# Attention values beside ones columns, grouped scores, and another order of the expert matmuls, in a fused attention and MoE kernel

## The chip, the cores and the metric

The kernel runs on one core of a Trainium2 chip. The metric is device time in microseconds of one execution, as the median of several runs. A profiled execution gives the trace; its span runs from the first to the last instruction, and its own time is the span with what lies around it.

## What is computed

Inputs are q, k, v of shape (4 batches, 8 heads, 768 positions, 64), two expert weights and two scalars. Attention is banded: each query sees the first 8 keys and the last 96 positions, with a distance bias per head. Its output, 3072 rows of 512, goes through one expert.

```python
scores = scale * q @ k.T                        # per batch and head
keep = (pos_k < 8) | ((rel >= 0) & (rel < 96))
scores = where(keep, scores - slope[h] * dist, -1e9)
a = exp(scores - max); a = a / (sum(a) + 1e-9)
x = (a @ v) as (3072, 512)
h = x @ w_in                                    # 512 x 2048
g = s * relu(h)**2 + b
out = g @ w_out                                 # 2048 x 512
```

## The kernel before, in words

The work is cut into 12 granules j of 256 rows (three per batch), and each granule into 4 head pairs: 48 units u. Only one core works; the order on each engine comes from the order of the program text, rearranged by a scheduler that lets ready work pass work that waits, mostly at the start.

A unit passes through three stages. `stage_T` (lines 204 and 212) transposes two 128-row blocks of k and of q on TensorE into one PSUM bank, and VectorE copies them to SBUF (line 222); lines 226 to 229 put together the key block that reaches back (`koff`). `stage_S` (line 268) computes scores with the 64-row half of each head, so that the two heads of the pair run side by side in the two halves of the array's rows; ScalarE takes the exponential (line 278) and VectorE multiplies by a template that holds bias and mask (line 282). The eight templates are made once by ScalarE (line 163) from `base` (lines 153 to 157). `stage_A` computes values (line 316) with 64 weight columns per head, the two heads side by side in the two halves of the array's columns, and then the row sums in the same way with a block of ones as the weights (line 329). ScalarE takes the logarithm of the sums and the exponential of its negative (lines 339, 341), and VectorE multiplies (line 342) into `xT`.

The expert runs in chunks on finished granules. `moe_p1` (line 355) makes 256 of the 2048 hidden columns with 8 matmuls of 256 columns; ScalarE applies relu (line 363), VectorE squares (line 364) into `gT`. `moe_p2` (line 389) is half of a 128-row output block, 8 matmuls of 512 columns; after the second half VectorE applies s and the bias vector (line 398) and SP stores. The bias vector is b times the column sums of w_out: `emit_bvec` (line 371) sums them with 16 matmuls by ones.

The main loop has one step for each unit: scores of the next unit, a first-layer chunk, values of this unit, another chunk, transposes of the unit after next, half an output block. The first layer lags one granule, the second two. PSUM has 3 banks for scores, 2 for values, 3 shared by transposes, both expert layers and the bias vector.

All loads are on the POOL queue and cast f32 to bf16. Their order is: q, k, v of granule 0 (line 80), w_in in four parts (line 92), granule 1, w_out in four parts (line 98), granule 2, and one later granule per four steps. Eight transfers of this queue may be under way; the ninth waits for the first. VectorE makes `voff` (lines 192, 194) once per granule, the V block that reaches back.

Of the kernel before, what the change touches and what calls it, by code (L numbers as in the profile page):

```python
# [8 lines left out]
F32 = mybir.dt.float32  # L9
BF16 = mybir.dt.bfloat16  # L10
ACT = mybir.ActivationFunctionType
ALU = mybir.AluOpType
# [5 lines left out]
def kernel(  # L18
# [13 lines left out]
    nc = tc.nc  # L32
    P = nc.NUM_PARTITIONS

    B, H, S, D = q.shape
    NG = int(n_global)
    NL = int(n_local)
    DM = H * D
    DF = moe_w_in.shape[1]
    GB = 2  # L40
    GT = GB * P
    NGR = S // GT
    HP = H // 2
    KC = DM // P
    FC = DF // P
    NJ = B * NGR
    NU = NJ * HP
# [7 lines left out]
    const = ctx.enter_context(tc.tile_pool(name="const", bufs=1))  # L55
    ldp = ctx.enter_context(tc.tile_pool(name="ldp", bufs=2))
    qkp = ctx.enter_context(tc.tile_pool(name="qkp", bufs=2))
    work = ctx.enter_context(tc.tile_pool(name="work", bufs=3))
    ppool = ctx.enter_context(tc.tile_pool(name="ppool", bufs=8))
    gpool = ctx.enter_context(tc.tile_pool(name="gpool", bufs=2))  # L60
    xpool = ctx.enter_context(tc.tile_pool(name="xpool", bufs=3))
    ps_sc = ctx.enter_context(tc.tile_pool(name="ps_sc", bufs=3, space=bass.MemoryType.PSUM))
    ps_av = ctx.enter_context(tc.tile_pool(name="ps_av", bufs=2, space=bass.MemoryType.PSUM))
    ps_h = ctx.enter_context(tc.tile_pool(name="ps_h", bufs=3, space=bass.MemoryType.PSUM))

    nc.scalar.preload_act_table_set("natural_log_exp_and_others")


    nat = {}
    for b in range(B):  # L70
        for nm in ("q", "k", "v"):
            nat[nm, b] = None

    def load(nm, src, b, g, h0, nh):
        key = (nm, b)
        if nat[key] is None:
            nat[key] = ldp.tile([P, S // P, H, D], BF16, name=f"{nm}nat", tag=f"{nm}nat")
        t = nat[key]
        for sb in range(g * GB, (g + 1) * GB):
            nc.gpsimd.dma_start(  # L80
                t[:, sb, h0 : h0 + nh, :],
                src[b, h0 : h0 + nh, sb * P : (sb + 1) * P, :].rearrange("h p d -> p h d"),
            )

    w_in_bf = const.tile([P, KC, DF], BF16, name="w_in_bf")
# [13 lines left out]
            w_out_bf[:, i * w : (i + 1) * w, :], w_out_view[:, i * w : (i + 1) * w, :]  # L99
        )  # L100

    def load_granule(b, g, parts=1):
        n = H // parts
        for h0 in range(0, H, n):
            load("k", k, b, g, h0, n)
            load("q", q, b, g, h0, n)
            load("v", v, b, g, h0, n)

    s_bc = const.tile([P, 1], F32, name="s_bc")
    nc.sync.dma_start(s_bc[:], moe_s.to_broadcast((P, 1)))  # L110
# [2 lines left out]

    ident_bf = const.tile([P, P], BF16, name="ident_bf")
    make_identity(nc, ident_bf[:])
    ones_bf = const.tile([P, P], BF16, name="ones_bf")
    nc.vector.memset(ones_bf[:], 1.0)


    base = const.tile([P, 5, P], F32, name="base")  # L120
# [14 lines left out]
        fill=NEG_BIG,  # L135
# [9 lines left out]
        base=NL - 1,  # L145
        channel_multiplier=1,
    )
    load_granule(0, 0)
    for i in range(4):
        load_w_in(i, 4)  # L150

# [14 lines left out]
        tmpl.append(t)  # L166

    load_granule(0, 1)
    for i in range(4):
        load_w_out(i, 4)  # L170
    load_granule(0, 2)


    st = {}
    qk = {}
    xT = {}
# [8 lines left out]

    def make_voff(j):
        b, g = divmod(j, NGR)
        vn = nat["v", b]
        if g == 0:
            return  # L190
        vo = work.tile([P, GB, H, D], BF16, name="voff", tag="voff", bufs=2)
        nc.vector.tensor_copy(vo[:], vn[:, g * GB - 1 : (g + 1) * GB - 1, :, :])
        for i in range(GB):
            nc.vector.tensor_copy(vo[0:NG, i, :, :], vn[0:NG, 0, :, :])
        voff_tiles[j] = vo
# [45 lines left out]
    def stage_S(u):  # L241
# [43 lines left out]

        return mms, [lambda: post(0), lambda: post(1)]

    def stage_A(u):
        j, hp, b, g = unit(u)
        first = g == 0  # L290
        pts = st[u]["pt"]
        vn = nat["v", b]
        vo = None if first else voff_tiles[j]
        av = ps_av.tile([P, 4 * P], F32, name="ps_av", tag="av")
        if j not in xT:
            xT[j] = xpool.tile([P, KC, GT], BF16, name="xT", tag="xT")
        if first:
            dcol, ocol = (0, 1), (None, 2)
        else:
            dcol, ocol = (0, 3), (1, 2)  # L300

        def mms():
            for i in range(GB):
                for off in range(2):
                    c = (ocol if off else dcol)[i]
                    if c is None:
                        continue
                    for hi in range(2):
                        h = 2 * hp + hi
                        if not off:  # L310
                            vv = vn[:, g * GB + i, h, :]
                        elif first:
                            vv = vn[:, 0, h, :]
                        else:
                            vv = vo[:, i, h, :]
                        nc.tensor.matmul(  # L316
                            av[hi * D : (hi + 1) * D, i * P : (i + 1) * P],
                            lhsT=vv,
                            rhs=pts[hi][:, c * P : (c + 1) * P],
                            start=not off,  # L320
                            stop=bool(off) or ocol[i] is None,
                        )
            for i in range(GB):
                for off in range(2):
                    c = (ocol if off else dcol)[i]
                    if c is None:
                        continue
                    for hi in range(2):
                        nc.tensor.matmul(  # L329
                            av[hi * D : (hi + 1) * D, GT + i * P : GT + (i + 1) * P],  # L330
                            lhsT=ones_bf[:, 0:D],
                            rhs=pts[hi][:, c * P : (c + 1) * P],
                            start=not off,
                            stop=bool(off) or ocol[i] is None,
                        )

        def norm():
            lg = work.tile([P, GT], F32, name="lg", tag="lg")
            nc.scalar.activation(lg[:], av[:, GT : 2 * GT], ACT.Ln)  # L339
            rc = work.tile([P, GT], F32, name="rc", tag="rc")  # L340
            nc.scalar.activation(rc[:], lg[:], ACT.Exp, scale=-1.0)  # L341
            nc.vector.tensor_tensor(xT[j][:, hp, :], av[:, 0:GT], rc[:], ALU.mult)  # L342

        return mms, norm

    def moe_p1(j, fp):

        if j not in gT:
            gT[j] = gpool.tile([P, FC, GT], BF16, name="gT", tag="gT")
        g = gT[j]  # L350
        ps = ps_h.tile([P, 2, GT], F32, name="ps_1", tag="psh")
        for i in range(2):
            fc = 2 * fp + i
            for kc in range(KC):
                nc.tensor.matmul(  # L355
                    ps[:, i, :],
                    lhsT=w_in_bf[:, kc, fc * P : (fc + 1) * P],
                    rhs=xT[j][:, kc, :],
                    start=(kc == 0),
                    stop=(kc == KC - 1),  # L360
                )
        gs = g[:, 2 * fp : 2 * fp + 2, :]
        nc.scalar.activation(gs, ps[:], ACT.Relu)  # L363
        nc.vector.tensor_tensor(gs, gs, gs, ALU.mult)  # L364

    bvec = const.tile([P, DM], F32, name="bvec")

    def emit_bvec():
        ps = ps_h.tile([P, DM], F32, name="ps_b", tag="psh")
        for fc in range(FC):  # L370
            nc.tensor.matmul(  # L371
                ps[:],
                lhsT=ones_bf[:],
                rhs=w_out_bf[:, fc, :],
                start=(fc == 0),
                stop=(fc == FC - 1),
            )
        nc.vector.tensor_scalar_mul(bvec[:], ps[:], b_bc[:])

    po_cur = {}  # L380
# [26 lines left out]
            nc.sync.dma_start(out[t0 : t0 + P, :], o_sb[:])  # L407


    pend_loads = []  # L410
    for b in range(1, B):
        for g in range(NGR):
            pend_loads.append((b, g))

    def run_T(u):
        ops, evac = stage_T(u)
        for op in ops:
            op()
        evac()

    def run_S(u):
        mms, posts = stage_S(u)
        mms()
        for p_ in posts:
            p_()

    NSTEP = NU + 2 * HP
    run_T(0)
    run_T(1)
    run_S(0)  # L430
    for s in range(NSTEP):
        jm = s // HP
        qd = s % HP
        if qd == 0:
            if jm >= 0 and pend_loads:
                load_granule(*pend_loads.pop(0))
            if jm + 1 < NJ:
                make_voff(jm + 1)
        if s + 1 < NU:
            run_S(s + 1)  # L440
        if 1 <= jm <= NJ:
            moe_p1(jm - 1, 2 * qd)
        if s < NU:
            mms, norm = stage_A(s)
            mms()
            norm()
        if 1 <= jm <= NJ:
            moe_p1(jm - 1, 2 * qd + 1)
        if s + 2 < NU:
            run_T(s + 2)  # L450
        if s == HP + 2:
            emit_bvec()
        if 2 <= jm:
            moe_p2(jm - 2, qd // 2, qd % 2)


# [33 lines left out]
```

The softmax here doesn't subtract the row's maximum and nothing guards it: scores larger than these inputs give would overflow.

## Time and profile before

| what | us |
|---|---|
| median of 3 runs | 264.14 (263.92 to 265.49) |
| profiled execution, own time | 265.33 |
| its span | 263.5 |
| TensorE busy | 242.9 |
| VectorE busy | 152.7 |
| ScalarE busy | 144.7 |
| GpSimd busy | 71.1 |
| mean granted TensorE clock | 0.996 |

How to read it: PE is TensorE, PEld its weight loads, DVE VectorE, ACT ScalarE, POOL GpSimd, SP the store queue. A timeline line gives the start, the time that the merged instructions took, the engine, the line of the kernel, output and inputs with shapes, and a count; in brackets stands the idle time ahead and what ended it. The chain of waits follows the last instruction back, at each step to what released it. Matmuls overlap, so that their cost is read from the distance between starts and not from the duration of one.

### The profile page before, as it was taken

Reading aid. Unit: us, or ns where it says so; the run is one execution under the profiler, and the core shown is the slowest. Engines: PE = TensorE matmul, PEld = TensorE weight load, DVE = VectorE, ACT = ScalarE, POOL = GpSimd, SP = SyncE. Lnnn points to the kernel's source line nnn. Section 1 sums busy time; section 2 is a strip of 40 time slices with the busy share of each in tenths; the row PEclk is TensorE's granted clock in tenths of the full one; section 3 lists DMA queues with packets and bytes.
Section 4 is the critical chain, followed back from the end, with each engine's and each line's share of the span. In section 5 each row is a group of like instructions: output and inputs, shape, how many; then the busy total and the mean of one; then the engine's idle time right before and its main releaser. Section 6 shows DMA issues by size and latency. Waiting matters only on the chain.

```text
span 263.5 us, 5861 instructions
## 1 busy us (share of the span) xinstructions
PE 242.9 (92%) x2376; PEld 155.4 (59%) x2416; DVE 152.7 (58%) x441; ACT 144.7 (55%) x297; POOL 71.1 (27%) x89
## 2 busy tenths in 40 slices
PE   0573999999999999999999999999999999999993
PEld 0352565756666566666666666656666566666641
DVE  2440746777856676577575676567657567543331
ACT  4770454857557476575665756646556466463310
POOL 9945649859910000069700000000000000000000
PEclk9999999999999999999999999999999999999998
DMA  6999999999991100159990110110011011011112
GB/s 43 145 206 167 206 182 155 151 110 141 160 141 40 44 29 14 40 36 164 179 106 0 44 40 2 40 42 21 21 40 44 0 42 44 0 42 40 40 42 80
DMA packets 82875, 20.31 MB, mean 77 GB/s; under 512 B 75680, under 2 KB 79776, under 8 KB 82848
## 3 DMA queue, kind: packets, MB, share of 16 engines
q0 software_dynamic: 79104, 13.64, 69.3%
q1 hardware_dynamic: 3744, 6.29, 6.5%
q8 instruction: 19, 0.31, 0.5%
q14 instruction: 8, 0.07, 0.1%
HBM read 27.26 MB, written 6.29 MB: 127 GB/s over the span
## 4 chain that ended last, share of the span: by engine, by line
PE 89%; DMA 5%; POOL 3%; issue 1%; DVE 0%; ACT 0%; POOLq 0%
PE ps_s L268 6%; PE ps_av L316 6%; DMA knat<-in_k_dram 5%; PE ps_av L329 4%; PE ps_t L204 2%; PE ps_t L212 2%; PE ps_3986 L389 1%; PE ps_4006 L389 1%; PE ps_3944 L389 1%; PE ps_3006 L389 1%; PE ps_1081 L389 1%; PE ps_b L371 1%; PE ps_2048 L389 1%; PE ps_3880 L389 1%; PE ps_3793 L389 1%; PE ps_3642 L389 1%
## 5 line engine op out<-in xcount | busy, mean ns | idle before, releaser
L278 ACT ACTIVATE pt<-ps_s 128x512 bf16<-128x512 f32 (+1 forms) x96 | 49.0, 559 | 70.2 <-PE ps_s L268 70.1
L355 PEld LDWEIGHTS <-w_in_bf 128*128 128x128 bf16 x768 | 69.4, 100 | 18.4 <-issue 1.4
L389 PEld LDWEIGHTS <-gT 128*128 128x128 bf16 x384 | 36.0, 98 | 35.0
L364 DVE TENSOR_TENSOR gT<-gT 128x512 bf16<-128x512 bf16 x96 | 40.7, 424 | 22.8 <-ACT gT L363 21.0
L80 POOL DMA_DIRECT2D knat<-in_k_dram x24 | 21.9, 930 | 47.4 <-PE ps_t L212 44.1
L342 DVE TENSOR_TENSOR xT<-ps_av,rc 128x256 bf16<-128x256 f32 x48 | 20.3, 422 | 13.7 <-ACT rc L341 13.7
L204 PE MATMUL ps_t<-ident_bf,knat 128*128 128x128 bf16 x96 | 14.5, 233 | 11.1 <-DMA knat<-in_k_dram 11.1
L222 DVE COPY qk<-ps_t 128x512 bf16<-128x512 bf16 x48 | 19.7, 415 | 7.9 <-PE ps_t L212 7.9
L80 POOL DMA_DIRECT2D vnat<-in_v_dram x24 | 21.2, 908 | 6.3 <-DMA w_in_bf<-in_moe_w_in_dram 2.6
L80 POOL DMA_DIRECT2D qnat<-in_q_dram x24 | 21.5, 913 | 0.4 <-issue 0.3
L341 ACT ACTIVATE rc<-lg 128x256 f32<-128x256 f32 x48 | 20.0, 416 | 1.4
L316 PE MATMUL ps_av<-pt,vnat 128*64 128x128 bf16 x224 | 19.6, 241 | 1.2 <-DVE pt L282 0.7
L268 PEld LDWEIGHTS <-qk 64*128 64x128 bf16 x224 | 7.6, 97 | 21.1 <-issue 16.2
L339 ACT ACTIVATE lg<-ps_av 128x256 f32<-128x256 f32 x48 | 18.4, 383 | 2.5 <-PE ps_av L329 2.5
L329 PE MATMUL ps_av<-pt,ones_bf 128*64 128x128 bf16 x352 | 19.5, 230 | 0.0
L268 PE MATMUL ps_s<-qk 64*128 64x128 bf16 x224 | 17.8, 233 | 0.3 <-DVE qk L222 0.3
L204 PEld LDWEIGHTS <-knat 128*128 128x128 bf16 x96 | 9.5, 102 | 13.5 <-DMA knat<-in_k_dram 11.6
L316 PEld LDWEIGHTS <-vnat 128*64 128x64 bf16 x224 | 10.7, 114 | 11.1 <-issue 10.6
L212 PE MATMUL ps_t<-ident_bf,qnat 128*128 128x128 bf16 x96 | 14.3, 234 | 1.3 <-DMA qnat<-in_q_dram 1.3
L329 PEld LDWEIGHTS <-ones_bf 128*64 128x64 bf16 x352 | 14.1, 118 | 0.0
L226 DVE COPY koff<-qk 128x120 bf16<-128x120 bf16 x32 | 7.3, 234 | 8.9 <-PE ps_s L268 8.9
L282 DVE TENSOR_TENSOR pt<-pt,tmpl_136 128x512 bf16<-128x512 bf16 (+1 forms) x12 | 4.8, 403 | 11.5 <-ACT pt L278 11.5
(284 smaller groups left out, 389.7 us busy)
## 6 DMA issues: line engine op xcount, KB each, us to landing
out_dram<-o_sb SPq DMA_DIRECT2D x24, 256.0 KB, 2.0
knat<-in_k_dram POOLq DMA_DIRECT2D x24, 128.0 KB, 6.5
qnat<-in_q_dram POOLq DMA_DIRECT2D x24, 128.0 KB, 6.5
vnat<-in_v_dram POOLq DMA_DIRECT2D x24, 128.0 KB, 6.7
w_in_bf<-in_moe_w_in_dram POOLq DMA_DIRECT2D x4, 512.0 KB, 9.9
w_out_bf<-in_moe_w_out_dram POOLq DMA_DIRECT2D x4, 512.0 KB, 10.7
s_bc<-in_moe_s_dram SPq DMA_DIRECT2D x1, 0.5 KB, 2.8
b_bc<-in_moe_b_dram SPq DMA_DIRECT2D x1, 0.5 KB, 2.9
```

The costliest lines, as they stand in the source:

```text
L80: nc.gpsimd.dma_start(t[:, sb, h0 : h0 + nh, :], src[b, h0 : h0 + nh, sb * P : (sb + 1) * P, :].rearrange("h p d -> p h d"),)
L204: lambda i=i: nc.tensor.transpose(ps[:, (GB + i) * P : (GB + i + 1) * P], kn[:, g * GB + i, 2 * hp : 2 * hp + 2, :], ident_bf[:],)
L222: nc.vector.tensor_copy(t[:], ps[:])
L268: nc.tensor.matmul(pss[hi][:, oc * P : (oc + 1) * P], lhsT=kt[r0 : r0 + D, kc0 : kc0 + P], rhs=t[r0 : r0 + D, qc0 : qc0 + P], start=True, ...
L278: nc.scalar.activation(pts[hi][:, 0:ncol], pss[hi][:, 0:ncol], ACT.Exp, scale=QSCALE)
L316: nc.tensor.matmul(av[hi * D : (hi + 1) * D, i * P : (i + 1) * P], lhsT=vv, rhs=pts[hi][:, c * P : (c + 1) * P], start=not off, stop=bool( ...
L329: nc.tensor.matmul(av[hi * D : (hi + 1) * D, GT + i * P : GT + (i + 1) * P], lhsT=ones_bf[:, 0:D], rhs=pts[hi][:, c * P : (c + 1) * P], st ...
L341: nc.scalar.activation(rc[:], lg[:], ACT.Exp, scale=-1.0)
L342: nc.vector.tensor_tensor(xT[j][:, hp, :], av[:, 0:GT], rc[:], ALU.mult)
L355: nc.tensor.matmul(ps[:, i, :], lhsT=w_in_bf[:, kc, fc * P : (fc + 1) * P], rhs=xT[j][:, kc, :], start=(kc == 0), stop=(kc == KC - 1),)
L364: nc.vector.tensor_tensor(gs, gs, gs, ALU.mult)
L389: nc.tensor.matmul(po[:], lhsT=gT[j][:, fc, tb * P : (tb + 1) * P], rhs=w_out_bf[:, fc, :], start=(fc == 0), stop=(fc == FC - 1),)
```

## The change

1. Values. V of a batch goes to a buffer with 192 columns per head pair: the first head's 64, 64 of ones (written once), the second head's 64. One matmul per head and block takes 128 of these columns as weights, so that values and row sums come out of one full-array matmul, in opposite halves for the two heads. ScalarE's logarithm and VectorE's multiplication become two instructions of 64 partitions each per unit. The value bank is a single one; there are 4 score banks. V arrives in two half transfers for each block, and `voff` has 1536 columns instead of 1024.
2. Scores of two units stand together in one step of two units.
3. q and k of granule 0 come by SP as f32, and VectorE casts them. w_out is loaded behind granule 2.
4. The column sums of w_out are made by VectorE: four reductions, two additions, then one f32 matmul by ones.
5. The expert chunks are spread over six places of a step. The second layer lags three granules, `gT` has 4 buffers, and the remaining chunks run at the end.

```diff
+    def load_qk_first(nm, src, sb):
+        f = work.tile([P, H, D], F32, name="first", tag="first", bufs=2 * GB)
+        nc.sync.dma_start(f[:], src[0, :, sb * P : (sb + 1) * P, :].rearrange("h p d -> p h d"))
+        nc.vector.tensor_copy(nat_tile(nm, 0)[:, sb, :, :], f[:])
+    for vb in vbuf:
+        nc.vector.memset(vb[:, :, :, D : 2 * D], 1.0)
...
     load_granule(0, 1)
+    load_granule(0, 2)
     for i in range(4):
         load_w_out(i, 4)
-    load_granule(0, 2)
...
+        for hi in range(2):
+            vc = slice(hi * D, hi * D + 2 * D)
             for i in range(GB):
+                nc.tensor.matmul(
+                    av[:, hi, i * P : (i + 1) * P],
+                    lhsT=vn[:, g * GB + i, hp, vc],
+                    rhs=pts[hi][:, dcol[i] * P : (dcol[i] + 1) * P],
+                    start=True,
+                    stop=ocol[i] is None,
+                )
...
+        for hi in range(2):
+            nc.scalar.activation(
+                lg[hi * D : (hi + 1) * D, :],
+                av[(1 - hi) * D : (2 - hi) * D, hi, :],
+                ACT.Ln,
+            )
+        rc = work.tile([P, GT], F32, name="rc", tag="rc")
+        nc.scalar.activation(rc[:], lg[:], ACT.Exp, scale=-1.0)
+        for hi in range(2):
+            r = slice(hi * D, (hi + 1) * D)
+            nc.vector.tensor_tensor(xT[j][r, hp, :], av[r, hi, :], rc[r, :], ALU.mult)
...
+    def emit_wsum(i):
+        n = FC // NW
+        nc.vector.tensor_reduce(
+            wsum[:, i, :],
+            w_out_bf[:, i * n : (i + 1) * n, :].rearrange("p f c -> p c f"),
+            axis=mybir.AxisListType.X,
+            op=ALU.add,
+        )
...
     def emit_bvec():
         ps = ps_h.tile([P, DM], F32, name="ps_b", tag="psh")
-        for fc in range(FC):
-            nc.tensor.matmul(
...
+        nc.vector.tensor_tensor(
+            wsum[:, 0:2, :], wsum[:, 0:2, :], wsum[:, 2:4, :], ALU.add
+        )
+        nc.vector.tensor_tensor(wsum[:, 0, :], wsum[:, 0, :], wsum[:, 1, :], ALU.add)
+        nc.tensor.matmul(ps[:], lhsT=ones_f[:], rhs=wsum[:, 0, :], start=True, stop=True)
         nc.vector.tensor_scalar_mul(bvec[:], ps[:], b_bc[:])
...
+    for j in range(NJ):
+        fill[j] = []
+        if j == 1:
+            fill[j] = p1_chunks(0)
+        elif j == 2:
+            fill[j] = p1_chunks(1)
+        elif j >= 3:
+            fill[j] = mix(p1_chunks(j - 1), p2_chunks(j - 3))
+    last = p1_chunks(NJ - 1)
+    for j in range(NJ - 3, NJ):
+        last += p2_chunks(j)
...
+        for u in (2 * s + 2, 2 * s + 3):
+            if u < NU:
+                mms, po_ = stage_S(u)
+                mms()
+                posts += po_
+        for i in range(2):
+            for p_ in posts[2 * i : 2 * i + 1]:
+                p_()
+            moe()
+            for p_ in posts[2 * i + 1 : 2 * i + 2]:
+                p_()
+            stage_A(2 * s + i)
+            moe()
+            if 2 * s + 4 + i < NU:
+                run_T(2 * s + 4 + i)
+            moe()
...
+    for s in range(NU // 2):
+        if s == 4:
+            for i in range(NW):
+                emit_wsum(i)
+        if s == 6:
+            emit_bvec()
+        step(s)
+    for c in last:
+        c()
```

## Prediction

> **What bounds the kernel now.** I read the page's busy shares first, then the chain of waits by engine.
>
> ```profile
> PE 242.9 (92%) x2376; PEld 155.4 (59%) x2416; DVE 152.7 (58%) x441; ACT 144.7 (55%) x297; POOL 71.1 (27%) x89
> ...
> PE 89%; DMA 5%; POOL 3%; issue 1%; DVE 0%; ACT 0%; POOLq 0%
> ```
>
> TensorE is the bound; loads matter only at the start. Next TensorE's timeline, for one steady unit and then for the start.
>
> ```profile
> 144.00 0.29 PE L268 MATMUL ps_s<-qk 64*128 64x128 bf16 x4
> ...
> 144.33 1.05 PE L355 MATMUL ps_2308<-xT,w_in_bf 128*128 128x256 bf16 x8
> 145.31 0.25 PE L316 MATMUL ps_av<-pt,vnat 128*64 128x128 bf16 x2
> ...
> 145.56 0.39 PE L329 MATMUL ps_av<-pt,ones_bf 128*64 128x128 bf16 x8
> 145.88 1.05 PE L355 MATMUL ps_2342<-xT,w_in_bf 128*128 128x256 bf16 x8
> 146.76 0.27 PE L204 MATMUL ps_t<-ident_bf,knat 128*128 128x128 bf16 x2
> ...
> 146.99 1.89 PE L389 MATMUL ps_2364<-w_out_bf,gT 128*128 128x512 bf16 x7
> 148.81 0.29 PE L268 MATMUL ps_s<-qk 64*128 64x128 bf16 x4
> ```
>
> ```profile
> 23.36 0.39 PE L204 MATMUL ps_t<-ident_bf,knat 128*128 128x128 bf16 x2 [4.56 <-DMA knat<-in_k_dram]
> ...
> 30.21 1.25 PE L355 MATMUL ps_468<-xT,w_in_bf 128*128 128x256 bf16 x5
> ...
> 39.84 0.50 PE L355 MATMUL ps_539<-xT,w_in_bf 128*128 128x256 bf16 x3
> ...
> 44.00 1.89 PE L371 MATMUL ps_b<-w_out_bf,ones_bf 128*128 128x512 bf16 x8
> 45.83 0.28 PE L268 MATMUL ps_s<-qk 64*128 64x128 bf16 x4
> ```
>
> A steady unit is 148.81 - 144.00 = 4.81 us without a gap: scores 0.33, first-layer chunk 0.98, values and sums 0.57, chunk 0.88, transposes 0.23, half an output block 1.82. A chunk in a row takes 0.87 and a half block 1.73 (the chain's sums for eight); four transposes give 0.056 for a 128-column matmul, so eight scores in pairs are 0.22. What is over stands where the array's split changes: 0.09 into scores (1.82 - 1.73), 0.11 out of them (0.33 - 0.22), 0.11 into values (0.98 - 0.87). Sixteen value and sum matmuls, in pairs, are 8 places of 0.071, not 0.056. At the start the second granule's k lets TensorE go on at 23.36; 256-column matmuls are about 0.21 us apart until 39.6 and 0.11 after, though the granted clock reads 1.00 all through. From 45.83 TensorE is dense.
>
> **Part by part, TensorE first.** Values: 704 half-array matmuls become 352 full-array ones. I cost each at the transposes' 0.056, which also have a new 128-column weight each. With 16 in a unit (32 units) 0.57 + 0.11 becomes 0.45; with 12 (16 units; 0.45 + 0.11 at 140.62) it becomes 0.34. That is 32 x 0.23 + 16 x 0.22 = 10.9 us. If the full-array form is no faster than the pairs, only the 0.11 goes: 48 x 0.11 = 5.3.
>
> [...]
>
> Scores: 48 blocks become 24 in the scheduler's steady order, so 24 x 0.20 = 4.8. Column sums: 16 matmuls of 512 columns (1.73 for eight: 3.46) against one with f32 operands. No f32 matmul is in the trace; between one bf16 row (0.22) and all sixteen (3.46) I take 0.9, the middle by ratio. That saves 2.6. TensorE saves 10.9 + 4.8 + 2.6 = 18.3 us in all.
>
> New waits in the steady step. The value bank is now one: the next unit's values wait for Ln, Ln, Exp, two multiplications. The rows:
>
> ```profile
> 144.43 1.09 ACT L278 ACTIVATE pt<-ps_s 128x512 bf16<-128x512 f32 x2 [1.68 <-PE ps_s L268]
> 145.42 0.60 ACT L363 ACTIVATE gT<-ps_2308 128x512 bf16<-128x512 f32 x1
> 145.99 0.38 ACT L339 ACTIVATE lg<-ps_av 128x256 f32<-128x256 f32 x1
> 146.40 0.42 ACT L341 ACTIVATE rc<-lg 128x256 f32<-128x256 f32 x1
> ...
> 146.85 0.42 DVE L342 TENSOR_TENSOR xT<-ps_av,rc 128x256 bf16<-128x256 f32 x1 [0.38 <-ACT rc L341]
> ```
>
> Count from the first score. The first exponential starts at 0.43 (144.43), four at 0.50 each are issued by 2.4; then comes a relu to 3.0, two Ln from 2.9, a relu, the Exp to 4.4, and two multiplications to 5.3. TensorE reaches the next values at 5.6, after scores 0.53, chunk 0.87, values 0.45, chunk 0.87, transposes 0.23, half block 1.73, chunk 0.87. That is 0.3 to spare. The half block at 2.95 needs the bank that the first relu frees at about 3.1: a wait of 0.15, in 12 steps 1.8 us. VectorE's second multiplication has the same column count as one had, so it is one more of 0.35 (146.85 to 147.20); voff grows by half of 0.45. Per step VectorE has about 7 of 8.9 us, so this is hidden; it surfaces when those 0.3 us are gone.
>
> **The start.** q and k of the first granule: SP's landing of 256 KB stores is 2.0 us in the page's issue list, so all four could be there by 0.73 + 3 x 0.34 + 2.0 = 3.8; taken as slowly as POOL's four of that shape (1.88 to 9.36 = 7.5) it is 8.2, beside V and w_in perhaps 10.3. I take 7.8. But VectorE's four casts stand ahead of the five base copies, so templates start not at 4.86 but near 9.7, and end near 14.8 instead of 10. This is hidden only because xT of granule 0 is not the next bound; the single value bank takes that granule's four units in series, from about 17, 0.65 for six values at the cold rate and 2.2 to 2.6 for what follows, and behind granule 1's transposes at 24: to about 32.5. The two memsets of ones (1536 columns; the old 128 took 0.17, so at most 2.0 each) end by 5.0, under the loads. s and b now wait on SP behind the four loads; nobody reads them before 60.
>
> Loads: POOL issues a q, k or v at 0.87 each (1.76 for two). Four fewer stand ahead of granule 1, so its k lands at 23.4 less 0 to 3.5, say 21; granules 1 and 2 (six each, V's halves counted as two) end 10.4 later, near 31; w_out, parts 2.5 apart by POOL's waits, from 34 to 43, and its first reader on VectorE comes near 38. The 24 more V issues lie in POOL's idle time (44 us ahead of knat). In the new order of VectorE the second voff stands ahead of later copies, so VectorE is held until 31.
>
> VectorE's ledger from there to the last addition for the column sums, by the instruction order of the changed kernel and distances between starts: 18 multiplications of xT at 0.35 = 6.3; 16 squares at 0.35 = 5.6; template products 10 x 0.35 + 4 x 0.27 = 4.6; 8 copies of qk at 0.39 = 3.1; 12 of koff at 0.10 = 1.2; voff 1.5; two additions 1.8; without reductions 24.1. A reduction reads 2048 elements and has no row. At voff's rate (1024 in 0.45) it is 0.9, at the output row's (512 f32 in 0.75) 3.0; I take the middle, 2.0, so 8.0. Sum 32.1: the one bias matmul, which all later TensorE work stands behind, comes at 31 + 32 = 63.
>
> [...]
>
> Bounds of 63: ScalarE's ledger from 14.8 (exponentials 12 x 0.39 + 16 x 0.50, Ln and Exp 12 x 1.18, relus 16 x 0.55: about 36) gives 51. Reductions of 3.0 with nine value blocks in series through one bank (0.9 + 2.6 each, from 32.5) and the reductions in between give about 74.
>
> **The sum.** Behind the bias matmul stand 80 chunks x 0.87 = 69.8; 48 half blocks x 1.73 = 82.9; 32 transposes x 0.23 = 7.4; 16 score blocks, 12 x 0.65 + 4 x 0.54 = 9.9; values 24 x 0.45 + 11 x 0.34 = 14.5; bank waits 1.8; the matmul 0.9; and the end as before, 263.5 - 259.4 = 4.1. That is 191.3. Span 63 + 191.3 = 254.3, 9.2 under 263.5. Before has 213.6 + 4.1 left at 45.83; the saving of 18.3 is thus half given back at the start. The profiled execution is 1.2 above the median (265.33 to 264.14), so I take the difference to the median: 264.14 - 9.2 = 254.9.
>
> **Rivals.** One: the start is covered. VectorE's reductions fall into its idle time, ScalarE's 51 holds, and the deferred second layer fills the end: 12 earlier, 243. For it, VectorE is only 58% busy; against it, its queue is in order and voff holds it. Two: the start is longer, 74: 266, no change. Three: the new values gain nothing beyond the 0.11: 5.6 less, 260.5; or they cost the pairs' 0.071 and the 0.11 stays: 10.9 less, 265.8. Four, the other side: the single value bank. If Ln sits behind exponentials and relus for 0.3 + 0.5 us longer than counted, 18 steps x 0.5 eat 9.2 and the gain is gone; at 1.2 longer it is 18 x 0.9 = 16, so 271, slower. For it, ScalarE gains 48 instructions; against it, it was idle 70 us waiting for scores.
>
> **How the numbers follow.** Chances: main case 0.57 (249 to 261), rival one 0.15 (243 to 249), two 0.12 (261 to 266), three 0.06 (260 to 266), four 0.10 (267 and more). The range 246 to 265 leaves out half of one, a little of two, and four: about 0.2. A measurement tells about 1% (2.6 us) from no change. Faster than 261.5: main, one and a little of the others, 0.74; within 1%: most of two and three, 0.16; slower: 0.10.
>
> **What would show it.** Right: value matmuls about 0.056 apart, score blocks of 16, steps of two units near 8.9 to 9.1 us instead of 9.6, the bias matmul near 63, reductions near 2 us in VectorE's queue ahead of xT. Wrong: idle TensorE time ahead of values released by VectorE's xT in each step; value matmuls 0.07 or more apart; bias matmul beyond 70 or before 55.

## The result and the profile after

The changed kernel takes 273.48 us (median of four runs, 272.04 to 274.74) against 264.03 for the kernel before beside it: a ratio of 1.0351, interval 1.027 to 1.0431. It is slower; 254.9 was forecast. The profiled execution took 272.04 us with a span of 270.2.

The page of the changed kernel, busy shares and then the chain of waits by engine:

```profile
PE 232.8 (86%) x2050; PEld 158.1 (58%) x2050; DVE 190.0 (70%) x501; ACT 158.8 (59%) x345; POOL 83.2 (31%) x109
...
PE 49%; POOL 13%; DMA 12%; DVE 11%; ACT 10%; issue 4%; POOLq 0%
```

TensorE has 10 us less to do (242.9 before) and the span is 6.7 longer. Before, 89% of the chain was TensorE's; now half of it is others'. The time did not go to TensorE's work but to its waits. There are two kinds. The first, in TensorE's timeline of one steady step of two units:

```profile
147.54 0.29 PE L292 MATMUL ps_s<-qk 64*128 64x128 bf16 x4
...
148.19 0.29 PE L292 MATMUL ps_s<-qk 64*128 64x128 bf16 x4 [0.25 <-DVE qk L246]
...
149.46 0.22 PE L330 MATMUL ps_av<-pt,vb_86 128*128 128x128 bf16 x1
...
149.91 1.04 PE L367 MATMUL ps_2224<-xT,w_in_bf 128*128 128x256 bf16 x8
...
151.01 1.89 PE L411 MATMUL ps_2246<-w_out_bf,gT 128*128 128x512 bf16 x8
...
156.97 0.28 PE L292 MATMUL ps_s<-qk 64*128 64x128 bf16 x4
```

Eight value matmuls take 0.45 us (149.46 to 149.91), 0.056 each, as forecast. But this step takes 9.43 (twelve steps take 9.30 each on the average), not 8.9 to 9.1: the second unit's scores start 0.65 behind the first's, since they wait for VectorE's copy of qk. VectorE's timeline ahead of the next step, whose second scores start at 157.51, shows why that copy is late:

```profile
155.68 0.86 DVE L356 TENSOR_TENSOR xT<-ps_av,rc 64x256 bf16<-64x256 f32 x2 [0.82 <-ACT rc L353]
156.57 0.43 DVE L376 TENSOR_TENSOR gT<-gT 128x512 bf16<-128x512 bf16 x1
157.03 0.42 DVE L246 COPY qk<-ps_t 128x512 bf16<-128x512 bf16 x1
```

TensorE's transposes are done at 155.3. The copy starts at 157.03, because in VectorE's queue it stands behind two multiplications that wait for ScalarE's reciprocal, and behind the square that follows them. In the kernel before the same queue left it early, 1.2 us ahead of its scores at 148.81:

```profile
147.20 0.42 DVE L222 COPY qk<-ps_t 128x512 bf16<-128x512 bf16 x1
```

The second kind of wait lies in the start. TensorE's timeline of the changed kernel from 49 us to the bias matmul:

```profile
49.94 0.50 PE L367 MATMUL ps_760<-xT,w_in_bf 128*128 128x256 bf16 x3
54.17 0.26 PE L330 MATMUL ps_av<-pt,vb_86 128*128 128x128 bf16 x1 [3.73 <-DVE xT L356]
54.23 0.31 PE L338 MATMUL ps_av<-pt,voff 128*128 128x128 bf16 x1
54.34 0.31 PE L330 MATMUL ps_av<-pt,vb_86 128*128 128x128 bf16 x1
...
58.23 0.28 PE L228 MATMUL ps_t<-ident_bf,knat 128*128 128x128 bf16 x2
...
72.92 0.27 PE L330 MATMUL ps_av<-pt,vb_87 128*128 128x128 bf16 x2 [2.01 <-DVE xT L356]
73.55 1.12 PE L399 MATMUL ps_b<-wsum,ones_f 128*128 128x512 f32 x2
```

and VectorE's in the same stretch:

```profile
49.63 3.62 DVE L386 TENSOR_REDUCE wsum<-w_out_bf 128x512 f32<-128x2048 bf16 x1
53.18 0.84 DVE L356 TENSOR_TENSOR xT<-ps_av,rc 64x256 bf16<-64x256 f32 x2
54.06 7.25 DVE L386 TENSOR_REDUCE wsum<-w_out_bf 128x512 f32<-128x2048 bf16 x2
61.23 0.40 DVE L306 TENSOR_TENSOR pt<-pt,tmpl_149 128x512 bf16<-128x512 bf16 x1
```

A reduction takes 3.65 us, over the upper bound of 3.0. xT at 53.18 stands behind one, TensorE's next values wait for it 3.73 us, and the template products stand behind the next two until 61.23. The bias matmul comes at 73.55 instead of 63. Behind it 196.7 us follow instead of 191.3. So of the 15.9 us by which the span misses (270.2 to 254.3), 10.5 lie ahead of the bias matmul and 5.4 behind it. Behind 74 us TensorE's marked waits are for the qk copy (2.2 us in ten waits) and for the `koff` copy (0.4 in one); it waits nowhere there for xT.

### The profile page after: what moved, and what is told of

Its sections match the earlier page's. It is cut to its first block, busy times and chain, and to the rows that moved or that the text cites. A ratio compares the mean times of both kernels' runs of the same rounds, so it can differ in the third digit from the quotient of the medians.

```text
span 270.2 us, 5323 instructions
## 1 busy us (share of the span) xinstructions
PE 232.8 (86%) x2050; PEld 158.1 (58%) x2050; DVE 190.0 (70%) x501; ACT 158.8 (59%) x345; POOL 83.2 (31%) x109
## 4 chain that ended last, share of the span: by engine, by line
PE 49%; POOL 13%; DMA 12%; DVE 11%; ACT 10%; issue 4%; POOLq 0%
DVE xT L356 5%; DMA w_in_bf<-in_moe_w_in_dram 5%; DMA w_out_bf<-in_moe_w_out_dram 5%; ACT lg L347 5%; POOL vb_86 L97 3%; POOL knat L83 3%; DVE qk L246 3%; ACT gT L375 3%; DMA vb_86<-in_v_dram 3%; DVE gT L376 3%; ACT rc L353 3%; PE ps_s L292 2%; POOL qnat L83 2%; POOL vb_87 L97 2%; PE ps_av L330 2%
## 5 line engine op out<-in xcount | busy, mean ns | idle before, releaser
L367 PEld LDWEIGHTS <-w_in_bf 128*128 128x128 bf16 x768 | 73.0, 100 | 17.9 <-issue 3.5
L302 ACT ACTIVATE pt<-ps_s 128x512 bf16<-128x512 f32 (+1 forms) x96 | 47.0, 565 | 21.5 <-PE ps_s L292 21.2
L356 DVE TENSOR_TENSOR xT<-ps_av,rc 64x256 bf16<-64x256 f32 x96 | 40.4, 421 | 21.6 <-ACT rc L353 20.9
L347 ACT ACTIVATE lg<-ps_av 64x256 f32<-64x256 f32 x96 | 36.4, 379 | 17.0 <-PE ps_av L338 15.5
L97 POOL DMA_DIRECT2D vb_87<-in_v_dram x24 | 18.5, 796 | 38.2 <-PE ps_av L330 21.0
L292 PE MATMUL ps_s<-qk 64*128 64x128 bf16 x224 | 16.6, 236 | 10.0 <-DVE qk L246 5.0
L97 POOL DMA_DIRECT2D vb_86<-in_v_dram x24 | 18.7, 838 | 7.0 <-DMA w_in_bf<-in_moe_w_in_dram 7.0
L330 PE MATMUL ps_av<-pt,vb_86 128*128 128x128 bf16 x96 | 14.4, 241 | 6.9 <-DVE xT L356 6.8
L338 PE MATMUL ps_av<-pt,voff 128*128 128x128 bf16 x128 | 18.5, 225 | 0.0
L386 DVE TENSOR_REDUCE wsum<-w_out_bf 128x512 f32<-128x2048 bf16 x4 | 14.5, 3652 | 0.0
L338 PEld LDWEIGHTS <-voff 128*128 128x128 bf16 x128 | 12.8, 100 | 2.4 <-issue 2.0
L330 PE MATMUL ps_av<-pt,vb_87 128*128 128x128 bf16 x96 | 12.4, 219 | 2.0 <-DVE xT L356 2.0
## 6 DMA issues: line engine op xcount, KB each, us to landing
w_in_bf<-in_moe_w_in_dram POOLq DMA_DIRECT2D x4, 512.0 KB, 10.5
```

Of the source, the lines that this page charges most:

```text
L97: nc.gpsimd.dma_start(vb[:, sb, :, 2 * hi * D : (2 * hi + 1) * D], pairs[hi, :, sb * P : (sb + 1) * P, :].rearrange("h p d -> p h d"),)
L292: nc.tensor.matmul(pss[hi][:, oc * P : (oc + 1) * P], lhsT=kt[r0 : r0 + D, kc0 : kc0 + P], rhs=t[r0 : r0 + D, qc0 : qc0 + P], start=True, ...
L302: nc.scalar.activation(pts[hi][:, 0:ncol], pss[hi][:, 0:ncol], ACT.Exp, scale=QSCALE)
L330: nc.tensor.matmul(av[:, hi, i * P : (i + 1) * P], lhsT=vn[:, g * GB + i, hp, vc], rhs=pts[hi][:, dcol[i] * P : (dcol[i] + 1) * P], start= ...
L338: nc.tensor.matmul(av[:, hi, i * P : (i + 1) * P], lhsT=vn[:, 0, hp, vc] if first else vo[:, i, hp, vc], rhs=pts[hi][:, ocol[i] * P : (oco ...
L347: nc.scalar.activation(lg[hi * D : (hi + 1) * D, :], av[(1 - hi) * D : (2 - hi) * D, hi, :], ACT.Ln,)
```

## The experiments

Theory A: the reductions stretch the start through VectorE's in-order queue. Theory E, added after the first four runs: the steady loss is the qk copy behind xT in that queue. Rivals: the single value bank (C), the longer chain behind the values whatever the order (F), the late first loads (B, D). Every run was timed beside the kernel before, which gave 264.0 to 264.4.

**Column sums back on TensorE.**

```
-        if s == 4: four emit_wsum(i)
-    two additions; one f32 matmul of wsum by ones
+    for fc in range(FC): nc.tensor.matmul(ps[:], lhsT=ones_bf[:], rhs=w_out_bf[:, fc, :], ...)
```

> The changed kernel with one part undone: the column sums of w_out are again 16 bf16 matmuls by ones on TensorE, and VectorE has no reductions and no additions for them. Theory A (the four reductions of 3.65 us hold VectorE's in-order queue, xT and the template products stand behind them, and TensorE waits through the value bank): the bias matmuls stand near 61 instead of 73.6, less by the 14.5 + 1.8 us taken off VectorE minus a few us that ScalarE then sets; TensorE has 2.5 us more to do (3.46 against 0.96); time about 273.5 - 12 + 2.5 = 264 (261 to 267). Rival B (the start is long because granule 0 and the loads come late, and the reductions lie in time that VectorE would wait anyway): the bias matmuls stay at 70 or later and the time is 273 to 276.

Measured 264.0 us (ratio 0.9978, 0.9938 to 1.0017). TensorE's timeline of this run:

```profile
62.04 3.62 PE L396 MATMUL ps_b<-w_out_bf,ones_bf 128*128 128x512 bf16 x16
```

The bias matmuls stand at 62.04, 11.5 earlier, though TensorE spends 2.6 more on them (3.55 to the next start instead of 0.96). A holds; B falls. Moving 3.6 us of TensorE's work to VectorE cost 9.5.

**Two value banks, three score banks.**

```
-ps_sc bufs=4, ps_av bufs=1
+ps_sc bufs=3, ps_av bufs=2
```

> The changed kernel with two value banks and three score banks instead of one and four. Theory A (VectorE's queue is the cause, the single value bank only the place where it shows): the reductions stay, TensorE's wait for xT ahead of the values goes, but the same time comes back as a wait for the template products or the qk copies; bias matmuls at 70 or later; the second scores of a step wait for a score bank; time 270 to 276. Rival C (the single value bank is the cause): the 8.8 us that TensorE waits for xT go, the bias matmuls stand near 65 and the time is 262 to 266.

Measured 279.0 us (1.0534, 1.0444 to 1.0625), worse than A allowed for. VectorE's timeline of this run:

```profile
45.08 14.34 DVE L386 TENSOR_REDUCE wsum<-w_out_bf 128x512 f32<-128x2048 bf16 x4
59.36 0.74 DVE L306 TENSOR_TENSOR pt<-pt,tmpl 128x512 bf16<-128x512 bf16 x2
60.02 0.85 DVE L356 TENSOR_TENSOR xT<-ps_av,rc 64x256 bf16<-64x256 f32 x2
```

In this schedule all four reductions stand in a row, and TensorE then waits 6.0 us at once for xT. The bias matmul comes at 72.63, not near 65 as C said: with 14.34 us of reductions in a row in VectorE's queue the second bank did not help, and C falls. The steady step is longer, 9.70 (83.73 to 190.47 in 11), and that is where this run loses. Two changes are in it, one value bank more and one score bank less, so its time alone says nothing against the single bank; the run with two banks below shows the same without the reductions.

**The values alone, in the kernel before.**

```
+V into vbuf beside ones columns (two half transfers), voff 1536 wide
-16 half-array value and sum matmuls, one Ln, one xT multiplication
+8 full-array matmuls, two Ln, two xT multiplications
```

> The kernel before with one part alone: the values in full-array mode beside ones columns (V in half transfers, two memsets, wider voff, two Ln and two xT multiplications a unit), with the order, the banks (two for values), the column sums and the first loads of before. If a value matmul of the full array takes 0.056 us and the 0.11 at the entry goes, as the changed kernel's trace shows: 264.0 - 10.9 = 253 (251 to 256). If the array split costs as much elsewhere (the entry of 0.11 moves to the scores' other side): 258 to 259. If the longer ScalarE and VectorE chain behind the values is no longer hidden: 262 or more.

Measured 279.0 us (1.0548, 1.0461 to 1.0635): a change that takes 8 us off TensorE's busy time costs 15. The waits of this run for TensorE:

```profile
PE ps_s L284 <- DVE qk L238: 19.5, 38, 1.1
```

(us in all, times, longest), and VectorE's timeline for one unit, whose scores start at 150.71 after 0.58 of waiting:

```profile
148.88 0.86 DVE L350 TENSOR_TENSOR xT<-ps_av,rc 64x256 bf16<-64x256 f32 x2 [0.81 <-ACT rc L347]
149.77 0.43 DVE L372 TENSOR_TENSOR gT<-gT 128x512 bf16<-128x512 bf16 x1
150.22 0.42 DVE L238 COPY qk<-ps_t 128x512 bf16<-128x512 bf16 x1
```

A unit takes 5.18 us (83.30 to 197.17 in 22 units), before 4.75. One more Ln and one more multiplication, both hidden by the count of busy time, push the qk copy past the moment at which its scores are due. This run has two value banks, no reductions and POOL's first loads: none of these can be its cause. That formed theory E.

**First q and k by POOL again.**

```
-load_qk_first (SP, f32, cast on VectorE)
+load_granule(0, 0) by POOL
```

> The changed kernel with the first q and k loaded by POOL again, converting as they go: no casts on VectorE ahead of the base copies. Theory A (the reductions and VectorE's queue from 31 to 73 set the length of the start): the first values come about 4 us earlier, but granule 1's k lands some 3 us later and the bias matmuls stay within 2 us of 73.6; time 271 to 276. Rival D (the late templates and granule 0 set it): bias matmuls near 69, time 268 to 270.

Measured 275.6 us (1.0413, 1.0341 to 1.0485), bias matmul at 75.05. The first values start at 12.84 instead of 18.33, and that does not matter while the reductions set the start: D falls. By the medians the first loads by SP are a gain of some 2 us; the intervals of the two ratios overlap.

**Transposes ahead of the values**, first in the kernel before with the values, then in the changed kernel, then there with the sums on TensorE. The lines of the changed kernel (in the kernel before it is `run_T(s + 2)`, set ahead of the values of unit s):

```
+            run_T(2 * s + 4 + i)
             stage_A(2 * s + i)
             moe()
-            run_T(2 * s + 4 + i)
```

> The kernel before with the full-array values, as in the run with the values alone, and the transposes of unit s+2 issued ahead of the values of unit s instead of behind them, so that VectorE's qk copy stands ahead of the two xT multiplications in its queue. Theory E (the values alone lost because the qk copy stood in VectorE's in-order queue behind xT, which waits for ScalarE's reciprocal: 0.58 us a unit): the 19.5 us that TensorE waits for the qk copy go, a steady unit is 4.81 - 0.23 = 4.58 us instead of 5.18, and the time is about 253 (250 to 257). Rival F (the longer chain of two Ln, Exp and two multiplications limits the unit whatever the order): the wait moves to another row, such as the values waiting for xT or the scores for a bank; a unit stays at 5.0 or more and the time at 272 or more.

Measured 259.63 us (0.9815, 0.9782 to 0.9847), 19.4 less than the values alone. TensorE's waits, the same line as above:

```profile
PE ps_s L284 <- DVE qk L238: 0.6, 2, 0.3
```

19.5 us of waiting became 0.6, by moving four transposes and nothing else. E holds, F falls. A unit is 4.59 us (82.02 to 196.80 in 25), near the 4.58 worked out. But 4.81 was one unit with sixteen value and sum matmuls; before's mean is 4.75, so the saving is 0.16 a unit and not 0.23. In every second unit the chunk behind the values starts 0.62 after the first value matmul (147.69 to 148.31), in the others 0.45 (152.44 to 152.89). The late one starts 0.04 after ScalarE's relu of the chunk before has ended (148.27); that it waits for that chunk's PSUM bank is read from these times and was not tested. Over 48 units the 0.07 is an estimated 3 us of the 6.6 by which 253 was missed. The rest fits the start, where TensorE was busy for 2.8 us less from 15 to 60 than before (36.5 to 39.3).

> The changed kernel with the transposes of each unit issued ahead of the values instead of behind them; the reductions and the single value bank stay. Theory E: the second scores of a steady step no longer wait for the qk copy; a steady step of two units is 9.0 instead of 9.43; over 18 to 20 steps 7 to 8 us less: 265.5 (263 to 269), the bias matmul still near 73. Rival F (the single value bank or ScalarE's chain is next behind the qk copy): step 9.3 or more, time 271 to 275.

Measured 268.06 us (1.0159, 1.012 to 1.0198), 5.4 less than the changed kernel. Twelve steps take 107.7 us (82.90 to 190.60; 8.98 each) instead of 111.6 (82.33 to 193.91; 9.30). The single value bank stayed: the steady loss was the order, not the bank. In the profiled executions the bias matmul comes 1.2 earlier (72.38), and 193.6 us follow it instead of 196.7, 3.0 less.

> The changed kernel with both: the column sums on TensorE again, and the transposes ahead of the values. If the two losses are separate, 264 - 7 = 257 (254 to 260). If the steady wait only moves elsewhere: 262 to 265.

Measured 259.75 us (0.9824, 0.9799 to 0.9849), 13.7 under the changed kernel; the two steps alone gave 9.5 and 5.4. They are nearly separate, and together ("both repairs" below) turn 3.5% slower into 1.8% faster. That is no faster than the kernel before with the values and the order alone (259.63): two units take 8.98 here and 9.18 there, but TensorE is busy for 33.0 us from 15 to 60 here and 36.5 there. What the other parts of the change gain in the steady step they lose in the start.

**The order alone, in the kernel before**, with no full-array values:

> The kernel before with the transposes ahead of the values and nothing else: a control for the run with the full-array values and that order. Before's TensorE waits only 0.3 us in all for the qk copy, so the order alone should bring nothing: 263 to 265. If the order itself were the gain: 260.

Measured 265.03 us (ratio 1.0, 0.9963 to 1.0038). The order is not a gain of its own: it only lets the values keep theirs.

**Reductions that read neighbours.**

```
-w_out_bf[...].rearrange("p f c -> p c f")
+w_out_bf[...] flat, "p (c f) -> p c f"
```

> The changed kernel with each reduction of 2048 elements into 512 sums reading four neighbouring elements instead of four that lie 512 apart (the sums are then other sums than the bias needs). If the 3.65 us of one reduction come from the stride: near 2.0 each, the bias matmul some 6 us earlier, time near 267. If they come from the operation's own rate on this form: 3.6 again, bias matmul near 73, time 272 to 275.

Measured 269.9 us (1.0214, 1.0169 to 1.0259). The reductions of this run, shortest, median and longest in ns:

```profile
L386 DVE TENSOR_REDUCE wsum<-w_out_bf x4: 2276/2278/2285, 40.6 to 54.8; 128x512 f32<-128x2048 bf16 x4
```

The same number of elements in and out: 2.28 us instead of 3.65. The stride of 512 elements costs 1.37 us a reduction. The bias matmul came 3.1 us earlier, 3.6 us off the time, less than the 5.5 us saved on VectorE and less than the 6 expected. This kernel does not compute the bias's sums; it only prices the stride.

**What is left of the start.** With both causes gone the bias matmuls still stand at 62.7. That run with the banks edited as above:

> The changed kernel with the sums on TensorE and the transposes first, and two value banks and three score banks instead of one and four. The run without this step has its bias matmuls at 62.7 though no reduction is left. Theory G (in the start, the single value bank sets the pace: value blocks stand 3.4 to 3.6 us apart at 35 to 58 us, each released by xT): with two banks they stand closer, the bias matmuls come near 56, as VectorE's own ledger without reductions gave (31 + 24.1), and TensorE's 4.4 us of waiting for xT go; in the steady step the fourth score block waits for a bank, some 0.3 a step; time 254 to 258. Rival H (VectorE's and ScalarE's queues set the pace and the bank is only where it shows): bias matmuls at 61 or later, time 260 to 265.

Measured 265.9 us (1.004, 1.0008 to 1.0073). Neither theory fits whole. TensorE's waits for xT went (4.4 us to none) and the bias matmuls came to 59.8, not near 56: with the second bank the start is 2.9 us shorter. The steady step lost more, 9.45 instead of 8.98. Its scores in TensorE's timeline:

```profile
148.09 0.29 PE L292 MATMUL ps_s<-qk 64*128 64x128 bf16 x4
...
148.32 0.27 PE L292 MATMUL ps_s<-qk 64*128 64x128 bf16 x2
...
148.64 0.50 PE L367 MATMUL ps<-xT,w_in_bf 128*128 128x256 bf16 x3
149.17 0.27 PE L292 MATMUL ps_s<-qk 64*128 64x128 bf16 x2
```

With three score banks the group is cut by part of a first-layer chunk, and the array's split changes twice more; how much of the 0.47 this is was not measured. With this order, one value bank and four score banks are the better choice of the two.

> The changed kernel with the sums on TensorE, the transposes first, and the second layer of a granule two granules behind, as in the kernel before, instead of three (bias matmuls two steps earlier). Theory I (with the second layer three granules behind, TensorE lacks work at 45 to 60 us while it waits for xT): its busy time in 45 to 60 goes from 11.0 towards 14 and the time to 255 to 257. Rival J (w_out lands only at 43 us and the second layer's first chunks wait for it, or the squares delay VectorE): no change, 259 to 261.

```
-            fill[j] = mix(p1_chunks(j - 1), p2_chunks(j - 3))
+            fill[j] = mix(p1_chunks(j - 1), p2_chunks(j - 2))
```

`emit_bvec` moves from step 6 to step 4 with it. Measured 258.05 us (0.9742, 0.9699 to 0.9785): with both repairs the later second layer costs 1.7. That lies between I and J: TensorE's busy time from 45 to 60 rose only from 10.97 to 11.96. What was left to wait for, TensorE's timeline and then VectorE's:

```profile
56.55 1.89 PE L414 MATMUL ps<-w_out_bf,gT 128*128 128x512 bf16 x8 [2.60 <-DVE qk L246]
```

```profile
54.01 0.82 DVE L216 COPY voff<-vb 128x1536 bf16<-128x1536 bf16 x1 [2.34 <-DMA vb<-in_v_dram]
...
56.09 0.41 DVE L246 COPY qk<-ps_t 128x512 bf16<-128x512 bf16 x1
```

Once more an early instruction of VectorE's queue waits, for V, and a qk copy behind it holds TensorE: the half block starts as the copy ends, and takes the bank that the copy frees.

> The changed kernel with the sums on TensorE, the transposes first, and the first q and k loaded by POOL again. Without the reductions the start shows what the first loads are worth. If the casts on VectorE ahead of the base copies cost as predicted (templates 5 us later, hidden by granule 1's k): with POOL's loads the first values come 4 us earlier, granule 1's k 2 us later, time 258 to 261. If the late templates reach the end: 254 to 257. If POOL's later loads do: 261 to 264.

Measured 260.95 us (0.9842, 0.9786 to 0.9897), 1.2 over the run with SP's first loads. The first values come 5.4 us earlier here (12.94 to 18.35) and the time is not shorter, as predicted: the late templates of SP's first loads are hidden, or at least outweighed, since the later loads by POOL are in the same run.

**V in one transfer, voff later, both** (on the run with the second layer two granules behind):

> The run with the second layer two granules behind, and V of a block in one transfer instead of two halves (each head's V beside its own ones columns, so that the destination has an even stride). Theory K (POOL's issues of the halves delay the loads of the start, and VectorE's voff copy and what is behind it wait for them): POOL's time falls by some 15 us, granule 1's k lands a little earlier, the wait of 2.34 us of voff goes, and the time is 254.5 to 256.5. Rival L (the transfers are paced by what the queue moves, 256 bytes a packet, not by POOL's issues): V lands as late as before, time 257.5 to 258.5.

> The run with the second layer two granules behind, and the voff copies of the next granule issued at the end of a granule's second step instead of at the start of its first, so that the template products no longer stand behind them in VectorE's queue. Theory M (VectorE's queue blocked by voff's wait for V is what holds TensorE 2.6 us at 56.6): that wait goes, time 255.5 (255 to 256.5). Rival: the copy is then too late for the next granule's values, which wait for it instead: 258 or more.

> Both edits together. If V's arrival was the limit and either edit removes it: as the better of the two, near 255. If POOL's issues and VectorE's blocked queue cost separately: 253 to 254.5.

```
-two half transfers of V
+one transfer; 256 columns per head pair: v, ones, v, 64 unused      (one V transfer)
-make_voff(j + 1) at the start of the first step
+make_voff(j + 1) at the end of the second     (late voff)
```

Measured 256.84, 256.37 and 256.87 us (ratios 0.9714, 0.9714, 0.9718, all within 0.964 to 0.979). With one transfer POOL's time fell from 83.0 to 67.8, voff's wait for V from 2.34 to 1.51 and TensorE's wait of 2.60 for the qk copy to 0.30; the time is just above K's range and under L's. With voff later voff's wait is 0.77, TensorE's wait of 2.60 is gone, and its busy time from 45 to 60 goes from 11.96 to 14.46; M holds. The two edits do not add, which fits one wait that either removes. They are worth 1.2 to 1.7 us by the medians; the intervals overlap that of the run they start from. These are the fastest kernels here, 2.9% under the kernel before.

## Why the prediction was wrong

**Right.** The value matmuls' price (0.056). Their saving was right in sign and too large: a unit of 4.59 against 4.75 is 0.16 where 0.22 to 0.23 was taken. The grouped scores: with both repairs sixteen take 0.55 and an entry of 0.10; twice eight take 2 x (0.33 + 0.10) = 0.86 in the kernel before with the values and the transposes first: 0.21 a step where 0.20 was taken. They were not run alone. The steady step of 8.9 to 9.1: 8.98, once the order lets it. The value bank in the steady step, "0.3 to spare": it holds, since in the changed kernel TensorE never waits for xT behind 74 us. The wait of 0.15 a step for the first relu's bank does not show there; with the transposes first one of 0.17 stands ahead of a chunk instead. The remainder behind the bias matmul: 258.1 - 62.7 = 195.4 in the run with both repairs, less 2.6 for the sums on TensorE 192.8, where 191.3 was summed.

**Wrong, first: "Per step VectorE has about 7 of 8.9 us, so this is hidden".** An engine was judged by its busy time. The figure was good (6.9 us busy in the step of 9.43 above), the conclusion was not. I followed the wait that the change adds (xT for the second Ln) to TensorE's values, but did not name what is queued behind that waiting instruction on VectorE: the square and the qk copy, which the next scores need; the wait for that copy was put at nothing. Issuing the transposes earlier brought 9.30 us a step to 8.98 and the time down by 5.4. It is chance that the sum also misses 5.4 us behind the bias matmul: 3.0 of these went with the new order (193.6 for 196.7), and 2.3 stayed.

**Wrong, second: the reductions.** 4 x 2.0 was taken, with 3.0 as the bound; they took 4 x 3.65 = 14.6, and the two additions 1.9. That is 6.6 of the 10.5 us by which the bias matmul came late, the largest single miss. The bounds came from rows with neighbouring elements; this one has a stride, and no row showed that. Taking the reductions, the additions and the f32 matmul out gave 9.5 us. In the run with neighbouring elements a reduction took 2.28, near the 2.0; the strided form took 3.65.

**Wrong, third: the ledger itself.** In the changed kernel the second voff starts at 31.83 (31 was taken), and from there to the last addition are 41.7 us where 32.1 were summed: 6.6 more for the reductions, 0.1 for the additions and 2.9 for everything else. Without the reductions and the additions it gives 31 + 22.3 = 53; the runs without them have 62.0 and 62.7. The ledger added instructions as if VectorE never waited. With both repairs VectorE is idle for 5.1 of the 30.5 us from 32.25 to the bias matmuls; its marked waits are 2.8 for ScalarE's relu, 1.4 for voff's V and 0.3 for the reciprocal. A second value bank brings the bias matmuls 2.9 earlier; the second layer's delay is worth 1.7 us of time, the blocked voff copy 1.2 to 1.7. How the 9 us split was not separated: the last runs change the order in which the bias matmuls come. The two repairs together leave 259.75, 4.9 over the forecast.

The fourth rival named 271 and slower, through the single value bank. The sign was right, and the mechanism was not: in the steady step TensorE waits for the qk copy and never for xT, and the step comes to 8.98 with the single bank kept.

## What to carry to other kernels

On an engine whose queue runs in order, as VectorE's did here (a qk copy whose transposes were done at 155.3 started at 157.03), ask for every added or lengthened wait which instruction stands behind it and when its reader is due; the busy share says nothing about it. An operation whose result another engine needs soon (here the qk copy) goes ahead of those that wait for a long chain, and moving it cost nothing (the order alone: ratio 1.0). Work given to an engine with idle time is only hidden if it is shorter than the time its neighbours in the queue can spare, whatever the idle time adds up to: here the sums, four reductions of 3.65 us and two additions on a VectorE that was busy for 58% of the span before, cost 9.5 us of time.

## What the runs showed of the hardware

In the changed kernel a pause cost more than itself: after 3.73 us without work TensorE's 128-column matmuls stand 0.107 us apart (54.23 to 54.34 above), and 0.056 apart only from about 58; the granted clock reads 0.50 from 55 to 57 there (0.89 over 45 to 60), and 1.00 over 45 to 60 in the run with the sums on TensorE. After a pause of 2.60 us (the second layer two granules behind) this was not seen: the half block behind it takes its 1.73 us (56.55 to 58.28), and the granted clock reads 1.00 over 45 to 60. But in the run with POOL's first loads and both repairs two pauses of 1.14 and 1.96 us, with a single transpose between them, were followed by the same 0.107:

```profile
47.16 0.23 PE L223 MATMUL ps_t<-ident_bf,knat 128*128 128x128 bf16 x1 [1.14 <-DMA knat<-in_k_dram]
49.35 0.29 PE L223 MATMUL ps_t<-ident_bf,knat 128*128 128x128 bf16 x1 [1.96 <-DMA knat<-in_k_dram]
...
50.49 0.31 PE L325 MATMUL ps_av<-pt,vb 128*128 128x128 bf16 x1
50.60 0.31 PE L333 MATMUL ps_av<-pt,voff 128*128 128x128 bf16 x1
```

The granted clock reads 0.50 there from 49 to 53 and 1.00 from 55 on (0.77 over 45 to 60), and the values at 55.56 stand 0.056 apart again. From which length of pause on this happens, these three cases do not show.

A reduction of 2048 bf16 elements took 2.28 us over neighbours and 3.65 over elements 512 apart.

POOL's issue of a V transfer took 0.80 us for half the block (64 KB) and 0.92 for the whole (128 KB): here the price goes by the transfer far more than by its size.
